# A fused linear attention and two feed-forward layers: products of halves for the second layer's second quarter, and a plain last group

## The chip, the cores and the metric

The kernel runs on one core of one Trainium2 chip. The metric is the device time of one execution in microseconds, from the profiler; several executions are timed and the median is taken. A core has TensorE (matrix products), VectorE (DVE), ScalarE (ACT), GpSimd (POOL), and SyncE (SP), which issues most transfers. Results of TensorE arrive in PSUM, eight banks of 512 columns of float32; all else is held in SBUF.

## The reference, cut to what matters

```
kv  = einsum('bhsd,bhse->bhde', k, v);  out = einsum('bhsd,bhde->bhse', q, kv)
out = out / sqrt(mean(out*out) + 1e-6) * g_norm          # 4 x 8 x 576 x 64
x   = out as 2304 tokens x 512
x   = softplus(x @ w_in1) @ w_out1                       # 512 -> 2048 -> 512
y   = elu(x @ w_in2) @ w_out2                            # 512 -> 2048 -> 512
```

All is float32. The weights come as float64 words and are rebuilt in the kernel.

## The kernel before, in words

**Numbers.** Every operand of a large product is held in two parts, a high one rounded to TensorE's fp32r type and a low one with the rest. A product is three matmuls: high x high, low x high and high x low. So each operand costs ScalarE a rounding copy and VectorE a subtraction.

**Tiling.** The 2304 tokens are six blocks of T = 384, taken as three pairs p. The hidden 2048 columns are four quarters q of four chunks of 128. A slot is two chunks for a pair (`slots`, 48 in all, 24 per layer), a group is the two slots of one quarter and pair. A group has a product into the hidden layer, an activation, and a product into the output, whose result is added to `acc_sb`.

**Products of halves.** A pair of blocks by two chunks is a 2 x 2 matrix of halves. The kernel forms it with seven products for eight (Strassen's scheme in Winograd's form): sums of operands are made beforehand, and three PSUM banks (A, B, C) collect the products. Into the hidden layer this is done almost everywhere (`product`, L874, products 1 to 7 of 6 matmuls of 384 columns each). Into the output it is done where `by_sevens(layer, q)` says so: before the change in the first layer from the second quarter on, in the second layer from the third on (SEVENS_FROM = 2). Elsewhere the output is plain (`slot_piece`, L1363 to L1365): in the second layer, 3 matmuls of 512 columns per chunk and tile of 128 tokens.

**A slot in sevens** (`slot_sevens`, L1117 to L1145, `part_sums`, L1157 to L1159). After the activation (`elu`, L1061 to L1081) h of the first block is split into x (768 columns, operands 1 and 2); of the second block x4 is split (384), S1 is formed, then three more sums of 384, and the two pairs of sums, xj and xk, are split (768 each). A plain slot splits only h of each block into G (768 each, `slot_parts`, L1322 and L1324).

**Output in sevens** (`out_piece`, L1216). Order of the products in the second layer: 1, 2, 6, 5, 3, 7, 4, each in two halves of rows m (two tiles, then one) and two slots f. A `fork` copies A into C (L1233, ScalarE). Six `flush` steps per half add a bank to `acc_sb` (L1250) or, in the last quarter, make the output o in one of three buffers q, which is sent out (L1248, L1258). Banks: A from a ring of two (`accA`), C and B from a ring of two (`accT`).

**Weights** (`conv`, L374 to L387; `split`, L404 and L408; `split_pair`, L460 to L466; `split_sums`, L474 to L483). A chunk is loaded, rebuilt and split; for products in sevens two chunks are combined: four VectorE operations of 256 columns, then two casts and two differences. The combined b12 takes the place of the original.

**The order.** It is written out by hand: the string TABLE names, step by step, a strand and the engine that takes its next step. Each engine runs its steps in the order of the list, so a wait on one engine holds all that the list puts behind it there. The strand `main` has the letters p (products into the hidden layer) and q (pieces into the output).

Of the kernel before, what the change touches and what calls it, by code (L numbers as in the profile page):

```python
# [17 lines left out]
P = 128  # L18
# [98 lines left out]
59p59p59p3qt3pt45t3pt46t47t3qt59p59p59p59p59p3pp3pa3pa59p48p3rt59p3qp48a3qa3qa59p59p48d59p3rt3st  # L117
3st00t48g59p59p3rp49p49a3ra3ra48d49d48p3sp4ap59p49g3tt3tt57t57t4ct4et4dt02t3ut4aa3sa3sa00a59p59p
59p4bp00a4ba59p59p49d4ad00d00d4bd00d59p49p4ag4bg59p59p59p59p3tp48a49a3ma3ta3ta01a59p59p59p59p4fp
3ut3vt02a4fa02a4ad5ad4bd01d4fd59p3vt3wt59p4bp4ap58p3up02d4fg3wt4ba4aa3ma3ua3ua3vp4gp02d02d4fd03a  # L120
4ga3va3va4fp3wp04t4jt03d4gd4fa3wa4gg4hp3wd5bd4ha04a4ip4ia04a58p4hd4hg4gd4id04d4gp4mp04d4hd4ig4ga
4ma4md04d4kt3xt3xt3yt3yt06t4qt4lt08t4np4hp4ha4na3ma06a06a59p59p4id4nd5cd58p3yp4ip58p4op4ia3ya3ma
5da5da05a5da4oa59p4mg4md06d3nd06d5ed06d05d3nd4od08a08a3ya07a4mp59p58p59p58p58p58p3zt3zt40t40t4rt
0at4ng4og40p08d4nd08d07d08d5dd4od3nd5ga40a40a09a5ga4np58p4up4tp4op58p58p58p0aa4ua4na0aa4ta4oa4ma
3na5ha3ma4pt0ct42t42t41t41t5at4ud09d0ad4td0ad58q4ug4tg0ad4ud5id4td58q58q58p58p4up3ma5ha0ca0ca4ua
0ba5ga42p4sp58p4sa58p5kd5jd0cd0bd42d0cd4sd0cd4sg0et5it44t43t44t43t42a5ha3na5la3na5la0ea0da0ea5hd
5md4sd5gd0ed0ed0dd4tp58q58q58p58p4sp58p4sa4ta3ma44p58p51t52t5bt0gt5mt53t0ed44d5od5nd44a58q54p55p
58q58q0fa54a3ma55a0fd54d54g5qd55d3nd5fd54d58q58q58q5pa55g58p58p58q54p58q0ga0ga5pa5la3na54a0gd55d
5sd5fd5fd5et5nt4vt58q55p56p58q58p58p5ra56a55a5pa5fa56d5ld0gd5wd56g58q4yp58q5va4ya56d4yd4yg58p56p
58p5ta5va5xa5ua5va56a0gd5pd5vd4yd4wt5st0jt5wt4xt0kt58p4zp58p4yp58q5fa0ja0ja4za4ya0ia5fa58q58q50p  # L130
58q5zd0jd4zd0jd50a0jd50d58q5ya5ya0ka0ka4zg50g60d4zd5fd0kd50d5zt60t0nt5kt5jt58q58p58p58q4zp58q58q
50p58q58p58p58q58q58q58q5fa4za50a3ma62a63a61a5ya58q0kd0kd65d66d3md3kd3md3md3kd3kd3kd5yd3kd3kd58q
58q58p67a64a3ma3ma3ma61a3ma68a68a3ma66t65t5qt58q58q58q58q6bd6ad68d6cd68d6dd3ld3md58q58q58q58q58q
58q58q58q58q58q6fa3ka6ga6ha69a58q58q58q58p58p61a3ma6ja58p58p58p6na6ia3ld3kd3ld6ed3ld6ld6kd3ld3ld
58p58p6pa6pa6oa3la58q58q58q58q58q61d6pd6pd0id3ld0hd0hd6rd6md0hd0hd58p58q58q58q6at6ct6dt6bt0ot3mt
6et6lt58q58p6qa6qa6qa6ta6ta0ha6ua58p58q58q58q58q58p58p6xa6sa6za6sa71a6qd6td0hd6wd6td6vd70d3mt3mt
3mt3mt58p58p0ma0na0na72a6ya58q58q58q58q58q58p58q58p0md6sd0nd0nd74d0nd0ld0ld76d0ld0ld75a73a73a73a
75a78a78a58p58p58p58q58q3mt3mt0rt78d75d78d0oa77a7aa0la0oa7ba79d73d58p58p58q0od0od7dd0ld0od58p58q
58q58p58q58q58q58q58q58p7ca77a7ca7ca0ra0ra7ea7ha77a7ga7ia0rd7cd0rd0rd7cd77d7jd0st3mt3mt0vt3mt3mt
58q58q58q58p58q0sa0sa7ka7la0qa77d0sd0sd77d0sd0qd0pd0pd77d0pd7fd0pd58p58p58q58q58q58q58q58p7oa7pa  # L140
77a7pa0pa7na7pa7na58q58q58q58q58p58p58q58q58q0wt3mt3mt3mt77d7qd0pd7nd7nd7pd7pd7ra0va7ka0va7ka0ua
7sa7ma7ta0vd0vd7kd0vd7md0ud58p58p58p58q58q0wa7ua0wa7va7za7ya80a7kd7kd0wd7xd0wd0wd0td7kd7wd58q58q
58p58q58p83a7ka82a84d0td0td7kd0td58q58p58q58p58p58q3mt0zt3mt86a7ta81a7ta85a85a0ta83a83a8aa8ag81d
87d85d85d0za0za89a58p58q58q58q58q8bd8cd0zd8dd0zd88d83d58q58p58q58q58p58q58q58q58q58q58p83d0td0zd
8hd8fd7td8id7td7td8kd7td8jd58q3mt10t8at3mt3mt58q58q58q8ga10a8ga10a8ea8ga0ya8ma89a8na58q58q58q58p
58p58p58q8ng7ta89a8la10d8gd10d8gd7td89d8ld8sd89d89d10d89d0yd8od8pa58q58q58p58p58q58q8qa8va89a8wa
8ua8xa0xd8rd89d0xd0xd0xd3mt3mt3mt13t58p58q58p58q58q58q58p8ya0xa8ya8ta8za8za93a91d90d92d8yd8yd0xd
8td58q58p58p58p58q58q58q58q58q58q58q58p13a13a12a95a96a8za8qa8qa9ba13d12d97d13d13d11d99d8zd94d11d
98d9ad8zd11d8qd8qd11d8qd8qd58q58p58q58q58q58q58p3mt3mt3mt3mt14t8nt9ea9ea9ca9ca8qa9fa9ga9gg58q58q
58p58q9hd9cd9cd9id9kd8qd58p58q58q14a14a9da95a95a14d14d9jd9md9dd95d14d58q58q58p58p58p58q58q3mt3mt  # L150
17t9gt9ea9pa9ra9la17a9qa9ed9nd9ed9od95d95d95d58p58q58q58q58p11a17a9sa9ua95a9ta9ta17d17d9vd95d9sd
17d11d58q58p58p58q58q58q58p58q58q3mt18t3mt9wa9la9la16a9za9xa18aa0a9ta18a9zg58q58q58p58q58p9ld16d
a1da2d18d9tda3d9yda4d9td18d9ld58p58p58q58q58q58q58q58q58q3mt3mt9zt3mt3mt1bt3mt9ld18d9lda8da7d15d
aada9d15d15d15da6aa0aa5a58q58q58q58q58q58q58p58p58q58p9laabaacaafa15aa6aacaa6aadd9ldabd15dacda6d
aeda6dacda0aaga1aaaha1ba1baaia1ada0d1bd1bd58q58p58p58qaigakaama3mt1ctaitajda0d1bda0da0d19d58q58q
58p58p58qaqd19d19d19dalaapaapaa0aanaaoaahaaraapaaraanda0dardard58p58p58p58q58q58q58qaha19aasa58q
58p58p58q58qava1ca1caayaawaawgapdahdaxd1cd1cd19dapdatdahdb0d1cd58q58p58q58q3mt3mt1ft3mt3mtawtb2d
58q58q58q58q58q58q58p1eab1aaua1fa1faazab1aahd1edb3db4d1fdb5d1fdahdb6d58q58q58q58q58p58q58qb1aaua
auab8ab9aahab7a1gt3mt3mtb9gb1db1daudbbdaud1fdahdaudaudb7dbaa1ga58p58q58q58p58q58q58p58pbga1gabca
bhaauabda1gdbed1gdbfd1gd1dd1dd1dd1dd58p58p58q58qb9t3mt1jtbiabkabmabjabja1dabldaudbjdbcd1ddbjd58p  # L160
58q58q58p58p58q58qbdabdabnabkaboa1ja1jabqabkabra58q58p58q58q58q58q58q58qbrgbta1iabdd1jd1jdbsdbkd
1idbvd1jdbudbpd1hdbkdbddbwd1hd1hd1hdbddbdd58q58p58p58p58q58q58q58q3mt3mt3mt3mt1kt3mt3mtbrtc0abxa
bzabxabda58q58q58p58qc1dc4dbxdbxdbddc6dc5d58q58q58p58p58p58q58q1kac0a1kabyabqabqa1hac7ac0acba1kd
1kd1kdbqdbyd1hdc2d1ntcbg58q58q58pcaac8accacda1nac3dc9dc0dc0dbqdbqdbqd58p58p58q58q58q1nachacfacea
bqa58q58q58pcgd1nd1ndbqdcedcid1ndc8acfac8acfacja1ma3mt1ot3mt58p58q58q58q58p58q58q58q58q58p1oa1oa
cqacfd1mdc8dcldcfdcmdcodcpdc8d1od1odckdc8d1od58q58q58q58q58q58p58p58p58q58q1ldc8d1ldcsd1ld1ldctd
3mt3mtcbt1rt3mt3mt3mt58q58qcvacnacuacyacyac8aczdcxdcydcwdcydc8d58q58q58q58q58pcra1ra1racna1lacna
d2acvad1a58p58p58q58p58qd0d1rd1ld1rdcrd1qad5acvad6a1rdcndd4d1qdcvd1pdcvdd5g58p58p58q58q58qd8ad3a
d9ad7adaad8a58p58qcnd1pdcndcnd1pd1pddbddcacnaddad8ad3adda58q58q58p58p58p58q1std5t3mt3mtdcdd8dcnd
ddddddd3a1padfa1sa1sadeadiadhadig58q58p58q58p58q58qdjad3d1sd1sd1sddkddgddmdd8dd3d1pd58p58p58q58q  # L170
58q58q58q58q58q58q1vt3mtdit3mt3mt3mtdodd3dd3ddqddpd58q3mt58q58q58qdnadna1ua1vadha1vadhadnadla1ud
dhd1vddrddsd1vddndduddnd1vddhddhd58q58q58q58q58q58p58p58pdxadyad3adtad3ddtddhddwadza58pdhae2adyg
dwd1tddvddhd1tde1d58p58p58q58q58q58p3oae0ae4ae4ae4ae5a1tde8d1tde4de7d58qe6ae9ae9ae3ae0ae0a58q58q
58q58p58q58q58pdyt1wte4d3ode9d3odecd3ode9dedde0deadebd58p58p58q58q58q58q58q58q58p1ta1wa3oa3oaefa
1waegaemdeldeed1wde0d1wdeidejdehd58p58p58q58q58q58q58qeka3oaena3oaepa3oaenae8temt1zte0derd1wdesd
eode0detd1tdeqaefae0aefa58p58q58q59p58qewd58q58q58p3odefde0dexdeyd58peqg58q1za1za1ya3oaeuaenaeva
# [57 lines left out]
def linear_attention_then_two_ffns(  # L234
# [857 lines left out]
    def slot_act(s, b, h, a):  # L1092
# [3 lines left out]
        if by_sevens(layer, q):  # L1096
            yield from slot_sevens(s, b, h, a)
            return
# [496 lines left out]
```

## Time and profile before

| | |
|---|---|
| runs | 790.48, 790.25, 790.72 us (median 790.48) |
| profiled execution | 790.45 us, its span from first to last instruction 788.7 us |
| TensorE clock granted | 1.00 throughout |
| TensorE, VectorE, ScalarE busy | 779.3, 663.7, 518.6 us |

How to read it: a busy time is the union of an engine's instructions. VectorE's and ScalarE's instructions overlap by some 0.08 us, so the spacing of starts is what one costs. Matmul ends are modelled; there too the spacing of starts counts. Windows give busy times per engine in a stretch, with the number of instructions in brackets.

### The profile page before, as it was taken

What the parts mean: (1) busy time and instruction counts of PE and PEld (TensorE: products, weight loads), DVE (VectorE), ACT (ScalarE), POOL (GpSimd) and SP (SyncE); (2) the same over time, 40 slices, a digit from 0 to 9 for tenths busy, and PEclk for the clock granted to TensorE, in tenths of its full rate; (3) what the DMA queues carried; (4) which work ended last, traced back from release to release, by engine and by line L of the source; (5) the groups of instructions that cost most, each with busy time, mean ns of one, the idle gap of its engine ahead of it and who ended that gap; (6) DMA issues with size and microseconds to landing.
All of it is one profiled execution on the core that took longest, in us unless ns stands there. A gap on an engine that the chain in (4) does not pass through costs nothing. (4 is left out here: it accounts for less than half of the span.)

```text
span 788.7 us, 13125 instructions
## 1 busy us (share of the span) xinstructions
PE 779.3 (99%) x4898; PEld 752.1 (95%) x4898; DVE 663.7 (84%) x1186; ACT 518.6 (66%) x984; POOL 57.1 (7%) x62
## 2 busy tenths in 40 slices
PE   8999999999999999999999999999999999999997
PEld 7899999999999999999998988998999999999996
DVE  3888887788889998999999996665778999999885
ACT  4877766676665676585677896765656767667551
POOL 3633500000000000000000000000000000000000
PEclk9999999999999999999999999999999999999999
DMA  9877799768678688779363879486674675685522
GB/s 321 292 269 294 250 376 319 276 241 290 223 232 301 212 279 288 242 227 309 121 215 143 284 294 322 173 301 224 216 254 154 247 254 180 262 293 181 174 81 86
DMA packets 49519, 191.30 MB, mean 243 GB/s; under 512 B 5296, under 2 KB 10928, under 8 KB 49456
## 3 DMA queue, kind: packets, MB, share of 16 engines
q1 hardware_dynamic: 47296, 184.57, 65.5%
q0 software_dynamic: 2160, 5.90, 4.1%
q8 instruction: 38, 0.62, 0.3%
q14 instruction: 25, 0.20, 0.1%
HBM read 146.80 MB, written 37.75 MB: 234 GB/s over the span
## 5 line engine op out<-in xcount | busy, mean ns | idle before, releaser
L874 PE MATMUL A<-x,wx 128*128 128x384 f32 x528 | 106.3, 335 | 0.0
L874 PE MATMUL A<-x,whi 128*128 128x384 f32 x352 | 99.9, 335 | 0.6 <-ACT hk L957 0.6
L874 PEld LDWEIGHTS A<-x,wx 128*128 128x128 f32 x528 | 92.4, 188 | 1.6 <-issue 0.3
L874 PEld LDWEIGHTS A<-x,whi 128*128 128x128 f32 x352 | 64.6, 188 | 1.4 <-ACT hk L957 0.9
L874 PE MATMUL A<-x,wlo 128*128 128x384 f32 x176 | 59.0, 335 | 0.0
L1365 PE MATMUL acc<-wlo,G 128*128 128x512 f32 x144 | 56.6, 393 | 0.0
L1364 PE MATMUL acc<-whi,G 128*128 128x512 f32 x144 | 56.6, 393 | 0.0
L1363 PE MATMUL acc<-whi,G 128*128 128x512 f32 x144 | 56.0, 389 | 0.0
L374 ACT ACTIVATE c<-raw 128x512 f32<-128x512 f32 x64 | 43.2, 675 | 17.4 <-DVE wx L480 8.7
L874 PE MATMUL B<-x,wx 128*128 128x384 f32 x264 | 53.0, 335 | 0.0
L874 PE MATMUL B<-x,whi 128*128 128x384 f32 x176 | 51.8, 335 | 0.0
L874 PE MATMUL C<-x,whi 128*128 128x384 f32 x176 | 51.8, 335 | 0.0
L408 DVE TENSOR_TENSOR wlo<-q,whi 128x512 fp32r<-128x512 f32 x64 | 44.0, 687 | 8.0 <-ACT whi L404 7.9
L874 PEld LDWEIGHTS B<-x,wx 128*128 128x128 f32 x264 | 46.2, 188 | 0.3
L387 DVE CUSTOM_DVE_ANT_0 q<-c,r 128x1024 uint16<-128x1024 uint16 x64 | 44.0, 687 | 1.4
L382 DVE SCALAR_TENSOR_TENSOR c<-raw,c 128x512 uint32<-128x512 uint32 x64 | 44.1, 689 | 1.0
L404 ACT CAST whi<-q 128x512 fp32r<-128x512 f32 x64 | 39.6, 619 | 7.5 <-DVE q L387 4.1
L377 ACT ACTIVATE r<-raw 128x512 uint32<-128x512 uint32 x64 | 42.9, 671 | 1.1 <-DVE wx L483 0.8
L1216 PE MATMUL A<-x,whi 128*128 128x384 f32 x144 | 41.7, 336 | 0.0
L834 DVE TENSOR_TENSOR x<-acc_sb,x 128x768 fp32r<-128x768 f32 x38 | 36.2, 954 | 3.4 <-ACT x L804 3.3
L902 PE MATMUL A<-x,whi 128*128 128x384 f32 x128 | 37.0, 344 | 0.0
L1290 POOL DMA_DIRECT2D acc_sb<-s x15 | 13.3, 887 | 326.2 <-ACT s L1275 219.6
(252 smaller groups left out, 2209.2 us busy)
## 6 DMA issues: line engine op xcount, KB each, us to landing
x<-spill SPq DMA_DIRECT2D x126, 768.0 KB, 6.5
raw<-w SPq DMA_DIRECT2D x64, 512.0 KB, 4.6
spill<-x SPq DMA_DIRECT2D x42, 768.0 KB, 6.1
acc_sb<-kv SPq DMA_DIRECT2D x16, 512.0 KB, 5.6
acc_sb<-s POOLq DMA_DIRECT2D x15, 384.0 KB, 5.5
out<-o SPq DMA_DIRECT2D x12, 256.0 KB, 2.2
q<-qt SPq DMA_DIRECT2D x9, 256.0 KB, 5.8
q_late<-qt SPq DMA_DIRECT2D x9, 256.0 KB, 3.5
```

Of the source, the lines that this page charges most:

```text
L374: nc.scalar.activation(c.bitcast(F32), high_f, AF.Copy, scale=2.0**-112)
L377: nc.scalar.activation(r, low, AF.Copy, scale=2.0**-29)
L382: nc.vector.scalar_tensor_tensor(c, high, 0x80000000, c, op0=ALU.bitwise_and, op1=ALU.bitwise_or)
L387: nc.vector.tensor_tensor(q.bitcast(U32), c, r, op=ALU.add)
L404: nc.scalar.copy(hi, q)
L408: nc.vector.tensor_sub(lo, q, f32(hi))
L874: nc.tensor.matmul(bank[:, :T], w, x, start=start and i == 0, stop=stop and i == len(seq) - 1, skip_group_check=True,)
L902: nc.tensor.matmul(a[:, :T], w, x, start=half == 0 and i == 0, stop=half == 1 and i == len(seq) - 1, skip_group_check=True,)
L1216: nc.tensor.matmul(a, l, r, start=first and k == i == 0, stop=last and i == 2, skip_group_check=True)
L1363: nc.tensor.matmul(a, l[0], r[0], start=(u == 0), stop=False)
L1364: nc.tensor.matmul(a, l[1], r[0], start=False, stop=False)
L1365: nc.tensor.matmul(a, l[0], r[1], start=False, stop=(u == QF - 1))
```

## The change

The second layer's second quarter goes in sevens too (SEVENS_FROM = 1), with its two weight pairs combined. The very last group (second layer, fourth quarter, third pair) is made plain for its output (`sevens_in`). Since that quarter's weights are combined ones, a new strand `right_again` restores the original right half of the first chunk from b11 and the sum b12 - b11, splits it again and writes it where product 4 of the group before had its operand. The plain pieces of the last group take their columns from both chunks' halves, so a tile of 512 columns is two times 3 matmuls of 256. The last tile's sum is made in two halves, as plain last groups are. The ring `accT` of two banks becomes `accT0` and `accT1` of one bank each, for the halves m of copies C and product 5. A branch in `flush_rows` could add sums by GpSimd's transfers, but its set BY_TRANSFER_2 is empty. The list is new throughout: 3698 steps for 3610, with 1234 for 1180 of VectorE and 1003 for 982 of ScalarE. From the first piece of the second layer's second quarter to the last of its third, VectorE has 349 steps in the new list and 311 in the old; for the third quarter alone the old list has 176. After the last product into the hidden layer the new list has 36 pieces: products 7 and 4 of the group before (8), then 28 of the last group.

```
-    SEVENS_FROM = 2
+    SEVENS_FROM = 1
+    BY_TRANSFER_2 = ()
-    BANKS = {"h": 2, "accA": 2, "accT": 2, "m": 1, "o": 1}
+    BANKS = {"h": 2, "accA": 2, "accT0": 1, "accT1": 1, "m": 1, "o": 1}
+    def sevens_in(layer, q, p):
+        return by_sevens(layer, q) and (layer, q, p) != (LAYERS - 1, NQ - 1, NPAIR - 1)
+    def right_again(f):
+        fc = NF - QF + 2 * f
+        need = [("w", LAYERS - 1, fc, 1), ("wx", LAYERS - 1, fc, 1)]
+        yield ((DVE, dve(256)),), [ring("cr"[f]), *need]
+        t, t_h = sbuf("cr"[f], 1, f"right{f}")
+        (lh, ll, *_), wx = w_t[LAYERS - 1, fc, 1], wx_t[LAYERS - 1, fc, 1][0]
+        nc.vector.tensor_add(t[:, :256], f32(lh)[:, :256], f32(ll)[:, :256])
+        yield ((DVE, dve(256)),), []
+        nc.vector.tensor_add(t[:, 256:], f32(wx)[:, 0, 0, :], f32(wx)[:, 1, 0, :])
+        yield ((DVE, dve(256)),), []
+        nc.vector.tensor_add(t[:, :256], t[:, :256], t[:, 256:])
+        hi, lo = w_t[LAYERS - 1, fc + 1, 1][:2]
+        yield ((ACT, act(256)),), [("four", f), ("w", LAYERS - 1, fc + 1, 1)]
+        nc.scalar.copy(hi[:, :256], t[:, :256])
+        yield ((DVE, dve(256)),), []
+        nc.vector.tensor_sub(lo[:, :256], t[:, :256], f32(hi)[:, :256])
+        drop(t_h)
+        mark("right", f)
...
-        sevens = by_sevens(layer, q)
+        sevens = sevens_in(layer, q, p)
...
-                5: [ring("accT")],
+                5: [ring(f"accT{m}")],
...
+            if (layer, q, p, o) == (LAYERS - 1, NQ - 1, NPAIR - 2, 4):
+                mark("four", f)
...
-            yield ((ACT, act(width, True)),), [ring("accT")]
-            banks["C", m] = psum("accT", f"C{n_}")
+            yield ((ACT, act(width, True)),), [ring(f"accT{m}")]
+            banks["C", m] = psum(f"accT{m}", f"C{n_}")
...
+        tag = ("accA", f"accT{(k // 2 + b * layer) % 2}")[k % 2]
+        if layer and by_sevens(layer, q):
+            need += [("w", layer, fc // 2 * 2 + 1, 1)] + [("right", f)] * (u % 2 == 0)
...
+            for n, x in enumerate(range(w0, w1, DM // 2)):
+                wh, wl = w_t[layer, fc // 2 * 2 + x * 2 // DM, 1][:2]
+                y = slice(DM // 2 * (u % 2), DM // 2 * (u % 2) + DM // 2)
+                to = a[:, n * DM // 2 : (n + 1) * DM // 2]
+                for v, (g_, w_) in enumerate(((l[0], wh), (l[0], wl), (l[1], wh))):
+                    nc.tensor.matmul(
+                        to, g_, w_[:, y], start=u == n == v == 0, stop=u == QF - 1 and v == 2,
+                        skip_group_check=True,
+                    )
...
-            if by_sevens(layer, q):
+            if sevens_in(layer, q, p):
                 yield from out_sevens(layer, q, p)
```

## Rows read from the trace of the kernel before

**Rows 1.** The page, busy time, share and instructions of each engine.
```profile
PE 779.3 (99%) x4898; PEld 752.1 (95%) x4898; DVE 663.7 (84%) x1186; ACT 518.6 (66%) x984; POOL 57.1 (7%) x62
```

**Rows 2.** Windows by stage of layer two: PE, PEld, DVE, ACT, POOL busy; clock, DMA.
```profile
430.00:522.00 92.00, 92.00 (x460) 82.92 (x460) 70.45 (x118) 71.40 (x132) 0.87 (x1) 1.00 0.75 265
522.00:614.00 92.00, 92.00 (x463) 83.44 (x462) 67.94 (x124) 53.27 (x101) 0.00 (x0) 1.00 0.64 228
614.00:703.00 89.00, 88.90 (x610) 87.69 (x610) 87.37 (x169) 63.45 (x119) 0.00 (x0) 1.00 0.67 243
703.00:785.00 82.00, 79.88 (x580) 78.25 (x578) 70.49 (x132) 41.35 (x76) 0.00 (x0) 1.00 0.41 140
...
500.00:600.00 100.00, 100.00 (x501) 90.32 (x500) 68.83 (x121) 62.47 (x118) 0.00 (x0) 1.00 0.64 226
640.00:720.00 80.00, 79.90 (x565) 79.41 (x564) 78.36 (x155) 54.39 (x101) 0.00 (x0) 1.00 0.63 229
```

**Rows 3.** Waits of TensorE from 30 us on: us, times, longest.
```profile
PE A L1216 <- DVE xj L1159: 0.7, 1, 0.7
...
PE A L1216 <- DVE o L1248: 0.4, 1, 0.4
```

**Rows 4.** Timeline of TensorE: start, us, instruction; 512, then 384 and 256 columns.
```profile
599.61 0.39 PE L1363 MATMUL acc<-whi,G 128*128 128x512 f32 x1
...
600.29 0.39 PE L1363 MATMUL acc<-whi,G 128*128 128x512 f32 x1
...
747.34 1.21 PE L874 MATMUL A<-x,wx 128*128 128x384 f32 x6
...
779.48 2.32 PE L1216 MATMUL A<-wx,xk 128*128 128x256 f32 x18
```

**Rows 5.** Timeline of TensorE at the end, with the idle time before and its releaser.
```profile
760.77 0.51 PE L874 MATMUL B<-x,whi 128*128 128x384 f32 x2
...
768.46 0.39 PE L1216 MATMUL A<-whi,x 128*128 128x256 f32 x1 [0.44 <-DVE o L1248]
...
772.55 2.45 PE L1216 MATMUL A<-wx,xj 128*128 128x256 f32 x16 [0.69 <-DVE xj L1159]
...
783.99 0.28 PE L1216 MATMUL A<-whi,x 128*128 128x256 f32 x1
```

**Rows 6.** Groups by line and form: xcount | busy us, mean ns | idle before.
```profile
L477 ACT CAST wx<-t 128x256 fp32r<-128x256 f32 x26 | 10.5, 404 | 0.9 <-DVE t L464 0.8
L466 DVE TENSOR_TENSOR q<-q,t 128x256 f32<-128x256 f32 x24 | 10.2, 423 | 0.4
L1233 ACT COPY C<-A 128x512 f32<-128x512 f32 x6 | 3.4, 573 | 1.9 <-PE A L1216 1.9
```

**Rows 7.** The chain that ended last, and VectorE's last sums in the timeline.
```profile
782.76 2.25 DMA out<-o
...
785.10 0.42 DVE o L1248
...
784.28 1.25 DVE L1248 TENSOR_TENSOR o<-acc_sb,A 128x512 f32<-128x512 f32 x2 [1.94 <-PE A L1216]
```

**Rows 8.** Timeline of VectorE, back to back: 768, 256, 512, 256 columns, then 384.
```profile
704.32 0.95 DVE L1119 TENSOR_TENSOR x<-hj,x 128x768 fp32r<-128x768 f32 x1
705.18 0.42 DVE L460 TENSOR_TENSOR t<-q,q 128x256 f32<-128x256 f32 x1
705.52 0.68 DVE L1250 TENSOR_TENSOR acc_sb<-acc_sb,A 128x512 f32<-128x512 f32 x1
706.12 0.42 DVE L462 TENSOR_TENSOR t<-q 128x256 f32<-128x256 f32 x1
...
707.12 0.55 DVE L1071 SCALAR_TENSOR_TENSOR hk<-e,A 128x384 f32<-128x384 f32 x1
707.58 0.42 DVE L466 TENSOR_TENSOR q<-q,t 128x256 f32<-128x256 f32 x1
```

**Rows 9.** Windows of 20 us, the turn from the first layer to the second.
```profile
420.00:440.00 20.00, 19.41 (x103) 17.77 (x102) 20.00 (x34) 17.64 (x33) 0.87 (x1) 1.00 0.37 112
```

More of the change, by code (lines that the diff above doesn't have):

```diff
@@ L1243, in flush_rows @@
             old = {3: [("s2", g, m)], 7: [("p5", g, m)]}.get(o, [])
+            if (q, p, o) in BY_TRANSFER_2 and m == 0:
+                yield ((ACT, act(width, True)),), [ring("f"), *old]
+                r, r_h = sbuf("f", 1, f"f{n_}_{o}")
+                r = r[:, :width].rearrange("p (t n) -> p t n", n=DM // 2)
+                nc.scalar.copy(r, x)
+                if name:
+                    mark(name, g, m)
+                if done:
+                    drop(x_h)
+                yield ((POOL, ADDS),), []
+                yield ((DMA, 2 * dma(P * width * 4)),), []
+                nc.gpsimd.dma_start(to, r, accum_op=ALU.add)
+                drop(r_h)
+                return
             yield ((DVE, dve(width)),), [ring("q"), *old] if ends else old
@@ L1348, in slot_piece @@
         fc = q * QF + u
-        tag = "acc" + "AT"[k % 2]
+        tag = ("accA", f"accT{(k // 2 + b * layer) % 2}")[k % 2]
         need = [("g", s, b), ("w", layer, fc, 1)] + [ring(tag)] * (u == 0)
-        yield ((PE, 3 * pe(w1 - w0)),), need
+        if layer and by_sevens(layer, q):
+            need += [("w", layer, fc // 2 * 2 + 1, 1)] + [("right", f)] * (u % 2 == 0)
+            yield ((PE, 3 * ((w1 - w0) // (DM // 2)) * pe(DM // 2)),), need
+        else:
+            yield ((PE, 3 * pe(w1 - w0)),), need
         gh, gl, G_h = g_t[s, b]
         hi, lo, hi_h, lo_h = w_t[layer, fc, 1]
+        halves = layer and by_sevens(layer, q)
         if u == 0:
@@ L1362, in slot_piece @@
             l, r = (gh[:, c], gl[:, c]), (hi[:, w0:w1], lo[:, w0:w1])
+        if halves:
+            for n, x in enumerate(range(w0, w1, DM // 2)):
[7 more added lines that the diff above has]
+                    )
+            if k == len(cut) - 1 and b == 0 and u == QF - 1:
+                mark("ended")
+            piece_done(s, b, f, k, u, i, w0, w1, cut, acc, left, G_h, layer, q, p)
+            return
         nc.tensor.matmul(a, l[0], r[0], start=(u == 0), stop=False)
@@ L1365, in slot_piece, with piece_done @@
         nc.tensor.matmul(a, l[0], r[1], start=False, stop=(u == QF - 1))
+        piece_done(s, b, f, k, u, i, w0, w1, cut, acc, left, G_h, layer, q, p)
+        if p == NPAIR - 1 and b == (layer == q == 0 and PLAIN == NPAIR) and k == len(cut) - 1:
+            drop(hi_h)
+            drop(lo_h)
+    def piece_done(s, b, f, k, u, i, w0, w1, cut, acc, left, G_h, layer, q, p):
         left[f] -= 1
@@ L1369, in slot_piece @@
                 drop(h)
-        if p == NPAIR - 1 and b == (layer == q == 0 and PLAIN == NPAIR) and k == len(cut) - 1:
-            drop(hi_h)
-            drop(lo_h)
         if u == QF - 1:
@@ L1531, in linear_attention_then_two_ffns @@
             order.add(AGAIN_KEY[f], pair_again(f))
+        for f in range(FP):
+            order.add(base(LAYERS * SLOTS - 2) + 1.5, right_again(f))
         for layer in range(LAYERS):
```

239 lines of the change are left out of this document (121 added, 118 removed).

## The prediction

> **What bounds the kernel now.** I read the busy times first: TensorE is busy for 99% of the span, VectorE for 84%, ScalarE for 66% [rows 1]. A busy TensorE need not be at its peak, so the windows by stage come next. The second layer's quarters run from about 430, 522, 614 and 703 us [rows 2]. In the first two, with plain products into the output, VectorE works 70.45 and 67.94 of 92 us; in the third, in sevens, 87.37 of 89, and TensorE still has no hole there (88.90 of 89). In the table of TensorE's waits the longest after the start is 0.7 us [rows 3], and what it loses lies mostly in the last 25 us: the fourth stage has 79.88 of 82 us. So the time is the number of columns that TensorE must stream, plus what it loses at the end; VectorE stands close behind.
>
> **The price of a matmul.** Starts of the 512-column matmuls of plain pieces are 0.23 us apart; three of them take 0.68 us, 0.227 each. Eighteen 256-column matmuls of sevens span 2.32 us, the last one's 0.28 included: 0.120 each. Six of 384 span 1.21 us, or 0.175, the last one's 0.34 included [rows 4]. Cost goes with columns.
>
> A plain group in the second layer has 2 blocks x 4 chunks x 3 tiles x 3 = 72 matmuls of 512: 16.3 us. A group in sevens has 7 products x 2 slots x 3 tiles x 3 = 126 of 256: 15.1 us. The windows agree: with its 84 matmuls into the hidden layer a plain group is 156, and 501 in 100 us make 31.1 us for one; a group in sevens is 210, and 565 in 80 us make 29.7 [rows 2]. The three groups of the second quarter gain 3 x 1.25 = 3.75 us. The last group becomes plain, but its pieces are cut in halves: 144 matmuls of 256 for 126, so 18 x 0.120 = 2.15 us more. **Columns: 1.6 us gained.**
>
> The Trainium skill, "TensorE: Matmul & The Clock Gate", section "Back-to-back issue gap", speaks against the change: it gives sustained spacings of about 81 ns for 128 columns and 131 ns for 512, so that long matmuls are the cheap ones. As an estimate from that page, on a straight line between, 256 columns would take 98 ns, a group 9.4 us plain and 12.3 us in sevens, and the columns' sum would be a loss of about 10 us. The rows have 0.227 and 0.120 us, so here the measured spacing decides and the page's does not apply.
>
> **The end.** After the last product into the hidden layer, which ends at about 761.1, TensorE still runs 165 matmuls of 256 (39 of the group before, 126 of the last one), and the last one starts at 783.99 [rows 5]. 165 x 0.120 is 19.7 us of the 23.0: 3.3 are lost. Two gaps have a name, 0.69 us for VectorE's split of the sums xj and 0.44 us for an output sum; the rest are small waits for sums that free a bank. With the last group plain these parts are not made: no x4, S1, three sums and two splits of sums per slot, and its matmuls need only G of a block. What takes their place is `right_again`: in the new list the plain group's first piece needs ("right", 0), which needs product 4 of the group before, half 0, then ScalarE's 256-column copy and VectorE's 256-column difference. A 256-column cast takes 0.404 us, a 256-column VectorE operation 0.42 [rows 6], and with a handover of about 0.1 after each the next piece starts 1.2 us after that product; the one piece left of product 4 covers 0.36 us. So 0.85 us stand free, and I allow 0.25 for a second wait; ends 0 (the list puts other ready pieces there) and 3.3 (as much as now). **2.2 us gained.**
>
> Then the tail. VectorE's last two sums wait for room in the three q buffers: one starts at 784.28 and the last not before the transfer of an earlier output lands at 785.01, so it starts at 785.10, 0.8 us behind the end of the last matmul (783.99 + 0.28) [rows 7]. In the plain group outputs come 2.9, 2.9 and 1.45 us apart (24 or 12 matmuls each), a transfer takes 2.25, and the buffer that the last one needs is free by then. **0.8 us gained**, ends 0 and 0.8.
>
> **VectorE in the second quarter.** Its prices are start to start: 768 columns 0.87 us, 512 0.60, 384 0.47, 256 0.335 [rows 8]. A plain slot has 6 operations of 384 (c22, c12, four of the ELU) and 2 of 768; a slot in sevens has 12 and 3. That is 6 x 0.47 + 0.87 = 3.7 us more, 7.4 a group. The six sums of 512 (3.6 us) become six of 512 and six of 256 (5.6). So a group costs 9.4 us more, three 28.3. The two weight pairs of the quarter, now combined, cost 2 x (4 x 0.335 + 0.60 + 0.335) = 4.6. Together 33 us, where VectorE works 67.94 of 92 us. That does not fit into 88.5 us; part must move to the neighbours, of which the first quarter has 21 us free. ScalarE gets two forks (one of 512 columns takes 0.57 us) per group and the combined weights' casts, against 39 us free [rows 2, 6].
>
> Unknown is what TensorE loses when VectorE is full for two quarters on end. From below: nothing. In the third quarter VectorE is 98% busy and TensorE loses 0.1 us. From above: a quarter in sevens needs 49.4 us for six slots, 16.9 for sums, 17.1 for eight weight chunks, 9.1 for four pairs and about 1 for copies, 93.5 in all against TensorE's 88.5, so 5 us a quarter and 10 in all if nothing moves. A row between: at 420 to 440 us VectorE is busy for all 20 us and TensorE is busy for 19.41, losing 0.6 us in plain sight [rows 9]. Between the first piece of the second quarter and the last of the third the new list has 349 VectorE steps; at the third quarter's 87.37 / 169 = 0.517 us a step that is 180.4 us beside 177 of TensorE. For the third quarter alone the old list has 176 steps, 91 us by the same price beside 88.5, and that excess of 2.5 was carried without a loss. The new excess is 3.4 over twice the time. I take **1.5 us lost**, nearer to the third quarter's row than to the inventory; ends 0 and 10.
>
> **Priced at nothing.** The banks: a ring of two handed round in one order becomes two rings of one, in the same order, so a copy and product 5 of the same half follow one another as before. The weights' transfers move the same bytes in shorter runs, with the DMA engines 64% busy in that stage; cover gone, a late chunk would show as ScalarE waiting on raw, and VectorE and then TensorE behind it. SP issues one output transfer fewer (23 for 24). The transfer branch for sums is not taken, its set is empty, so POOL's queue gets nothing. The new list may move anything else by some tenths either way.
>
> **Sum.** -1.6 - 2.2 - 0.8 + 1.5 = -3.1 us. The profiled execution took 790.45 us (span 788.7), against a median of 790.48, so the sum holds for both: **787.4 us**. A measurement can tell about 0.2%, 1.6 us, from no change.
>
> **The rivals.** (1) VectorE loses nothing: the list spreads its work into the first quarter. Then 785.9. The slack there and the third quarter speak for it, the 0.6 us at 420 against it. (2) VectorE becomes the bound, the other side: from the point where its lateness costs TensorE over 6.2 us (4.6 gained and 1.6 more) the kernel is slower. With the inventory's 10 us it is 790.5 - 4.6 + 10 = 796; at 7 it is 793. The place is the second quarter's end and the third, where the splits x, xj and xk come late and the input of each product waits. For it: 93.5 over 88.5 us in two quarters running. Against it: the list's 349 steps. The Trainium skill, "Perfetto Trace Analysis", section "Optimizing Scalar/DVE Operations", says that with VectorE saturated work should be offloaded to ScalarE; the change keeps all sums on VectorE, and what that costs no run here shows. (3) The same lateness costs 3 to 6 us and eats the gain: 789 to 791.5. (4) The end does not get shorter, since `right_again` waits for product 4 at the point where nothing else is ready: 787.4 + 2.2 = 789.6. That the change does less than it says I rule out: the pieces and their matmuls follow from the code.
>
> **Chances.** Forecast (a loss of 0.5 to 3 us at VectorE, 786.4 to 788.9) 0.41; rival 1 0.25; rival 3 0.15; rival 4 0.05; rival 2 0.14. Faster is the forecast and rival 1: 0.66. Within 0.2%: rivals 3 and 4, 0.20. Slower: 0.14. The range goes from 784.6 (rival 1 with the wait on `right` covered, and some tenths from the list) to 792.2 (rival 2's near edge).
>
> **What would show it.** Right: 256-column matmuls up by 3 x 126 + 144 - 126 = 396, 512-column ones down by 216; VectorE busy for 97% or more from 522 to 700 and TensorE windows there without holes of more than 1.5 us together; after the last product into the hidden layer 180 matmuls with about 1 us lost; a last sum that waits for a matmul and not for a transfer. Wrong: TensorE waiting for x, xj, xk or for a sum's bank all through the second and third quarters; a wait of over 2 us on whi behind `right_again`; a chain at the end that still runs over output transfers.

## The result, and the profile after

| | before | after |
|---|---|---|
| median (runs) | 790.48 us (790.25 to 790.72) | 797.15 us (796.90 to 798.69) |
| ratio, 95% interval | | 1.0086 [1.0071, 1.0102] |
| profiled execution, span | 790.45, 788.7 us | 796.90, 795.1 us |

The change makes the kernel slower, by 6.7 us (0.7 to 1.0%). First the page of the kernel after, its busy times, against [rows 1]; then its windows by stage, against [rows 2, 9] (same columns), with two short stretches at turns of quarters behind them.

```profile
PE 781.3 (98%) x5082; PEld 760.6 (96%) x5082; DVE 685.0 (86%) x1240; ACT 529.4 (67%) x1005; POOL 55.9 (7%) x62
```

```profile
430.00:522.00 92.00, 90.85 (x455) 81.89 (x456) 73.75 (x124) 70.27 (x132) 0.87 (x1) 1.00 0.78 278
522.00:614.00 92.00, 91.17 (x618) 89.11 (x617) 89.58 (x174) 66.85 (x125) 0.00 (x0) 1.00 0.64 240
614.00:703.00 89.00, 86.99 (x610) 85.83 (x609) 87.40 (x171) 62.66 (x118) 0.00 (x0) 1.00 0.57 204
703.00:785.00 82.00, 80.01 (x573) 78.38 (x572) 68.27 (x130) 42.72 (x79) 0.00 (x0) 1.00 0.46 168
...
420.00:440.00 20.00, 18.51 (x103) 17.43 (x102) 20.00 (x34) 16.36 (x31) 0.87 (x1) 1.00 0.64 221
616.00:628.00 12.00, 9.99 (x67) 8.86 (x66) 11.79 (x24) 10.14 (x19) 0.00 (x0) 1.00 0.41 153
716.00:724.00 8.00, 6.30 (x38) 5.44 (x38) 7.73 (x17) 5.77 (x10) 0.00 (x0) 1.00 0.35 106
```

VectorE now works 89.58 of 92 us in the second quarter (67.94 before), and TensorE, which had hardly a hole from 440 to 703 us, has them in every stage, 2.0 and 1.7 us in the two short stretches alone. Its waits from 30 us on (us, times, longest), which had no more than 0.7 us in one place [rows 3]:

```profile
PE A L1245 <- DVE acc_sb L1296: 2.1, 4, 1.0
PE A L903 <- ACT hk L986: 1.3, 1, 1.3
PE A L1245 <- DVE wlo L416: 0.9, 2, 0.6
PE A L1245 <- ACT whi L412: 0.8, 1, 0.8
PE A L903 <- ACT hj L986: 0.7, 2, 0.5
```

**Where the time went.** To place it, the pitches of [rows 4] are added up over all matmuls up to a moment (0.227, 0.172 and 0.120 us for 512, 384 and 256 columns; the shorter ones of the attention by their own pitch) and taken from the time of that moment; what is left is lost. "Streamed" is that sum at the end, and "760 on" stops at the last matmul's start. The pitches set the level of every column: with the mean spacings of back-to-back matmuls in these two traces (0.229, 0.174 and 0.119 us) some 5 us less is lost between 100 and 760 us in either, and 8.8 us lie between the two kernels where the table has 8.2. So the differences carry the argument, to some 0.6 us, and not the levels.

```
us lost            up to 100   100-420  420-460  460-520  520-600  600-700  700-760   100-760   760 on   streamed
before                 11.45      2.78     1.78     0.89     1.22     1.24     0.19      8.10     3.25      761.2
after                  14.59      2.84     3.21     1.00     2.10     3.80     3.34     16.29     1.00      759.6
```

The profiled executions differ by 6.45 us: columns -1.6, start +3.1, from 100 to 760 us +8.2, the end -2.25, and what follows the last matmul -1.0 (3.69 for 4.67 us). The gains are as forecast, though the columns' -1.6 is the forecast's own pitches times the counts (-2.3 by the mean spacings). The loss in the middle is over five times its term. By place it is 1.4 us from 420 to 460, 3.4 from 520 to 700, 3.2 from 700 to 760, and 0.2 in the rest.

How a hole of the middle comes about, at the turn into the third quarter: first the timeline of TensorE, then of VectorE.

```profile
615.77 1.84 PE L1245 MATMUL A<-wx,xk 128*128 128x256 f32 x14
...
619.09 0.28 PE L1245 MATMUL A<-whi,x 128*128 128x256 f32 x1
620.35 0.38 PE L1245 MATMUL A<-whi,x 128*128 128x256 f32 x1 [0.99 <-DVE acc_sb L1296]
```

```profile
616.94 0.69 DVE L1296 TENSOR_TENSOR acc_sb<-acc_sb,A 128x512 f32<-128x512 f32 x1 [0.21 <-PE A L1245]
617.54 0.42 DVE L468 TENSOR_TENSOR t<-q,q 128x256 f32<-128x256 f32 x1
617.88 0.55 DVE L1110 SCALAR_TENSOR_TENSOR hj<-e,hj 128x384 f32<-128x384 f32 x1
618.35 0.42 DVE L470 TENSOR_TENSOR t<-q 128x256 f32<-128x256 f32 x1
618.68 0.95 DVE L1188 TENSOR_TENSOR xj<-hj,xj 128x768 fp32r<-128x768 f32 x1
619.55 0.42 DVE L472 TENSOR_TENSOR t<-q,t 128x256 f32<-128x256 f32 x1
619.88 0.41 DVE L1296 TENSOR_TENSOR acc_sb<-acc_sb,A 128x256 f32<-128x256 f32 x1
620.22 0.42 DVE L474 TENSOR_TENSOR q<-q,t 128x256 f32<-128x256 f32 x1
```

TensorE has finished a piece by 619.4 and needs a bank A for the next; the bank comes free with the sum at 619.88. What that sum adds is there by about 617.6 (14 matmuls of 0.120 from 615.77, and the last one's 0.28), but it stands in VectorE's list behind five others, three of them (L468, L470, L472) of a weight pair that is being combined. After the first row none has idle time before it: VectorE does not rest, and the list decides who is late. The Trainium skill, "PSUM — Partial Sum Buffer", section "Engine vs sequencer instructions", says that VectorE's and ScalarE's queues are strictly first in, first out; the rows agree: a sum of 0.33 us waited for 2.3 us of other work ahead of it.

Not every hole is VectorE's alone. The longest wait of the table above, 1.3 us on the copy of hk (L986), ends at 430.7 us, at the turn between the layers, and names ScalarE; the waits on whi and hj name it too:

```profile
430.73 0.44 PE L903 MATMUL A<-x,whi 128*128 128x384 f32 x1 [1.30 <-ACT hk L986]
```

The end, against [rows 5, 7]: the timeline of TensorE (the last product into the hidden layer, the first and the last piece of the plain group), then VectorE's last sums.

```profile
768.70 0.51 PE L903 MATMUL B<-x,whi 128*128 128x384 f32 x2
...
773.98 0.35 PE L1421 MATMUL acc<-whi,G 128*128 128x256 f32 x1 [0.15 <-ACT whi L494]
...
791.44 0.28 PE L1421 MATMUL acc<-whi,G 128*128 128x256 f32 x1
```

```profile
790.32 0.42 DVE L751 TENSOR_TENSOR o<-acc_sb,acc 128x256 f32<-128x256 f32 x1 [0.75 <-PE acc L1421]
791.76 0.42 DVE L751 TENSOR_TENSOR o<-acc_sb,acc 128x256 f32<-128x256 f32 x1 [1.01 <-PE acc L1421]
```

### The profile page after: what moved, and what is told of

It is laid out like the page before. It is cut to its first block, busy times and chain, and to the rows that moved or that the text cites. A ratio compares the mean times of both kernels' runs of the same rounds, so it can differ in the third digit from the quotient of the medians.

```text
span 795.1 us, 13586 instructions
## 1 busy us (share of the span) xinstructions
PE 781.3 (98%) x5082; PEld 760.6 (96%) x5082; DVE 685.0 (86%) x1240; ACT 529.4 (67%) x1005; POOL 55.9 (7%) x62
## 4 chain that ended last, share of the span: by engine, by line
PE 86%; DVE 9%; ACT 1%; DMA 1%; issue 1%; SPq 0%; DVEq 0%
PE A L903 20%; PE A L1245 15%; PE B L903 10%; PE B L1245 8%; PE C L903 5%; PE A L931 4%; PE C L1245 4%; PE acc L1429 4%; PE acc L1431 4%; PE acc L1430 4%; PE acc L1421 2%; PE kv L579 1%; PE po L646 1%; PE warm L1546 1%; DVE x L863 1%
## 5 line engine op out<-in xcount | busy, mean ns | idle before, releaser
L1245 PE MATMUL A<-whi,x 128*128 128x256 f32 x192 | 39.9, 287 | 3.2 <-DVE acc_sb L1296 2.1
L986 ACT COPY hk<-A 128x384 f32<-128x384 f32 x37 | 17.7, 479 | 33.8 <-PE A L903 33.6
L1245 PEld LDWEIGHTS A<-whi,x 128*128 128x128 f32 x192 | 31.6, 189 | 5.5 <-DVE acc_sb L1296 3.6
```

The source lines that it names most:

```text
L1245: nc.tensor.matmul(a, l, r, start=first and k == i == 0, stop=last and i == 2, skip_group_check=True)
```

## The experiments

Each experiment had the kernel before beside it on the same chip; ratios are to that. The table gives for each profiled execution what it lost, as above. Four rows lose 0.19 to 0.21 us from 700 to 760 us; every kernel with the plain last group loses 1.2 us or more there.

```
us lost                        up to 100   100-520  520-600  600-700  700-760   100-760   median   before beside it
before                             11.45      5.45     1.22     1.24     0.19      8.10   790.48
after                              14.59      7.05     2.10     3.80     3.34     16.29   797.15   790.48
last group plain alone             14.04      5.44     1.27     0.92     1.21      8.84   791.36   790.61
old order up to 200 us             11.57      7.23     2.09     3.77     3.33     16.42   794.05   790.61
less work for VectorE              13.10     10.04     1.39     2.22     3.03     16.68   794.96   790.61
one ring of two banks              13.91      7.74     2.10     3.78     3.33     16.95   796.55   790.61
list c                             14.14      7.06     1.08     3.25     1.45     12.84   791.77   791.74
list d                             12.86      5.36     1.46     2.90     1.52     11.24   790.30   791.72
list d, less work                  11.52      5.12     0.37     0.69     1.39      7.57   785.95   791.72
before, 10 us more for VectorE     12.88      5.72     2.91     0.93     0.20      9.76   793.45   791.74
before, 21 us more                 14.55      5.40     7.47     2.74     0.20     15.81   800.31   791.74
before, 31 us more                 13.75      5.40    10.64     8.44     0.21     24.69   808.27   791.74
```

**The last group plain, alone.** TensorE's order of the kernel before up to the last 36 pieces, that of the change from there, and the banks in one ring. On VectorE and ScalarE the order departs from that of before earlier, from some 733 us on, and VectorE takes the first steps of `right_again` at 735 us.

```
-    SEVENS_FROM = 1
+    SEVENS_FROM = 2
-    BANKS = {"h": 2, "accA": 2, "accT0": 1, "accT1": 1, "m": 1, "o": 1}
+    BANKS = {"h": 2, "accA": 2, "accT": 2, "m": 1, "o": 1}
...
```

> The last group plain alone: the second layer's second quarter stays plain, accT is a ring of two again, the old list is kept up to the last 36 pieces and the new list's order is taken from there. If the end does what the two traces say (2.15 us more columns, 2.25 less lost after the last product into the hidden layer, 1.0 less after the last matmul), the time is 790.5 + 2.15 - 2.25 - 1.0 = 789.4 us. Rival: the shorter end is a gift of the emptier VectorE queue of the whole new list; then the columns alone count and the time is 791.5 to 792.6.

791.36 us, ratio 1.0004 [0.9995, 1.0014]. Its profile has the three parts as expected: 763.3 us streamed (+2.1), 0.99 lost from 760 us on (-2.26), 3.68 after the last matmul (-1.0), so -1.2. But it also loses 1.02 us more from 700 to 760 us, so that all these together come to -0.1, and in the median no gain shows: the interval, -0.4 to +1.1 us, excludes -1.2. The rival's 791.5 to 792.6 is nearer than the expected 789.4. In front of the holes, at 739.6, 741.3 and 748.1 us, VectorE's list has the first steps of `right_again`:

```profile
735.29 0.75 DVE L484 TENSOR_TENSOR right<-whi,wlo 128x256 f32<-128x256 f32 x2
```

That these steps cause the holes was not tested; a few copies changed places there as well.

**The old order at the start.** The changed kernel, the list of the kernel before for the first 200 us. In this run and that of one ring below some banks come to hold other sums than the reference's; all instructions and sizes are those of the change.

```
-    BANKS = {"h": 2, "accA": 2, "accT0": 1, "accT1": 1, "m": 1, "o": 1}
+    BANKS = {"h": 2, "accA": 2, "accT": 2, "m": 1, "o": 1}
-    TABLE (the list of the change)
+    TABLE (the list of before up to 200 us, then that of the change)
...
```

> The changed kernel with the old list's order for the first 200 us and the new order behind it; accT as a ring of two, since the old order hands its banks round in another way than one bank per half allows. If the 3.1 us that TensorE loses more in the first 60 us come from the new list's start, the time falls from 797.15 to 794 us, and the loss at 100 us from 14.6 to 11.5. Rival: they belong to the execution or the chip, and the time stays within 0.5 us of 797.

794.05 us, 1.0042 [1.0027, 1.0056], and the 3.1 us at the start were gone, as expected. By itself this run would put them down to the list. The table speaks against that: with the old order at the start eleven profiled executions (lists a and b below, which have no line in the table, among them) lost 11.45 to 14.55 us up to 100 us, with the new one three lost 13.10 to 14.59. The times of all executions lean the other way: the five of this run took 793.71 to 794.55 us, while the seven of the changed kernel and of the run with one ring, in the new order throughout, took 794.34 to 798.89, six of them over 796. Whether the new order makes a bad start more frequent stays open. What does stand: from 100 us on this run loses 16.4 us like the changed kernel, and with a start like that of before the change costs 3.4 us.

**Less work for VectorE.** In the second layer the low parts of the weights and of x, x4, xj and xk are products with nought, so they hold no low values; VectorE has some 30 us less. One of the six places, and the function that three of them call:

```
+    def low(s, to, h, hi):
+        if slots[s][0]:
+            nc.vector.tensor_scalar(to, hi, 0.0, None, op0=ALU.mult)
+        else:
+            nc.vector.tensor_sub(to, h, hi)
...
-        nc.vector.tensor_sub(parts[1], h, f32(parts[0]))
+        low(s, parts[1], h, f32(parts[0]))
...
```

> The changed kernel, same list, with some 30 us of VectorE work taken out of the second layer: the low parts of weights, x, x4, xj and xk are written as the high part times zero (one input, about half the time) and not as a difference, so the low parts are zero. If VectorE's load as such delays TensorE, the 9 us lost from 420 to 760 us fall below 3 and the time is 789 to 791 us. Rival: the order of the list does, at the turns from quarter to quarter, where steps wait for matmuls and rooms in front of steps that TensorE needs; then most of the loss stays and the time is 793.5 to 796 us.

794.96 us, 1.0048 [1.0029, 1.0067]. From 520 to 760 us it loses 6.64 us, for 9.24 in the changed kernel and 2.65 before. (Between 290 and 305 us it lost 3.6 us otherwise: 1.8 in a wait for a transfer of x, and most of the rest behind it at the lower level of the clock, 1.2 GHz for 2.4; the table's 16.68 has it.) So over a third of what the change loses there went with 30 us of VectorE's work, most of it from 600 to 700 us, and the rest stayed although VectorE was now free for some 12 us in each of the second and third quarters:

```profile
522.00:614.00 92.00, 91.82 (x623) 89.84 (x622) 79.40 (x177) 66.95 (x127) 0.00 (x0) 1.00 0.67 246
614.00:703.00 89.00, 88.23 (x621) 87.32 (x621) 77.68 (x174) 62.22 (x118) 0.00 (x0) 1.00 0.58 208
```

The time is the rival's (793.5 to 796). This is the stretch at the lower level, with the granted clock of 0.50:

```profile
296.00:299.00 3.00, 3.00 (x11) 3.00 (x10) 1.87 (x4) 1.28 (x3) 0.00 (x0) 0.50 0.47 194
```
 The part of the loss that stayed points to the order of the list.

**One ring of two banks.** The changed kernel and its list, with accT0 and accT1 as one ring again.

```
-    BANKS = {"h": 2, "accA": 2, "accT0": 1, "accT1": 1, "m": 1, "o": 1}
+    BANKS = {"h": 2, "accA": 2, "accT": 2, "m": 1, "o": 1}
...
```

> The changed kernel and its list with accT as one ring of two banks. If the split of the banks has a price of its own, the time falls by 1 us or more below 797. If a ring of two handed round in this list's order is the same as two rings of one, as the prediction priced it, the time stays at 796.5 to 798 us.

796.55 us, 1.0073 [1.0050, 1.0095], and the losses by stage are those of the changed kernel to 0.1 us from 460 us on. The split of the banks has no price that shows.

**Two searched lists, a and b.** With the banks of the change, and the transposed tile of the attention in the bank that the old order wants for it:

```
-            tag = ("accA", f"accT{nm // 2 % 2}")[nm % 2] if j < 3 else "om"[nm % 2]
+            tag = ("accA", "accT0")[nm % 2] if j < 3 else "om"[nm % 2]
...
-            yield from late(nm, bank, po_h, x, tag)
+            yield from late(nm, bank, po_h, x, "accT1" if tag == "accT0" else tag)
-    TABLE (the list of the change)
+    TABLE (the list of before up to 200 us, then a searched order)
```

> The changed kernel with another list: the order of the kernel before for the first 200 us, and from there an order searched for this kernel, in which the weights' conversions of the second layer are taken earlier and the sums of products stand ahead of them. Every operation of the changed kernel is still made, on the same engines but for some ten steps; the banks stay one each. VectorE's load from 520 to 702 us is as in the changed kernel. Theory (the list, not the load): the losses of the changed kernel at the start (3.1 us), at the turn between the layers (1.5) and in the second to fourth quarters (7.7, against 2.65 in the kernel before) mostly go: 785 to 788 us. Rival (a VectorE that is full for two quarters on end costs TensorE, whatever the order): only the start is won back, 793 to 794.5.

> As the run beside it, with a third order of the same steps, reached from another start of the search. It says how far one list differs from another. Theory (the list, not the load): within 2 us of the run beside it, 785 to 789 us. Rival (the load): 793 to 795.

830.15 us, 1.0478 [1.0444, 1.0512], and 818.10 us, 1.0317 [1.0302, 1.0333]: the theory and the rival of either run miss by far. The waits of ScalarE between 220 and 780 us, first in list a, then in list b and in the kernel before:

```profile
ACT c L382 <- DMA raw<-w: 66.7, 21, 6.8
```

```profile
ACT c L382 <- DMA raw<-w: 60.0, 19, 6.0
```

```profile
ACT c L374 <- DMA raw<-w: 7.0, 3, 3.8
```

Both lists convert a weights' chunk right behind the issue of its transfer, which lands some 5 us later. The page of list a, its DMA issues (count, KB each, median us from issue to landing):

```profile
raw<-w SPq DMA_DIRECT2D x64, 512.0 KB, 5.0
```

ScalarE stands there, and all that the list puts behind it stands too.

**List c.** The same edit, with an order in which each transfer has its time.

> Again the changed kernel with another list and every operation of it (the list of the kernel before for the first 200 us, three steps of VectorE more and three of ScalarE fewer than in the changed kernel). The two lists tried so far took the weights' chunks too soon after their transfers were issued: ScalarE waited 66.7 us for raw, where the kernel before has 7.0. This list leaves every transfer 2.7 us beyond its own length before its reader's place. VectorE's work between the stages is moved by a few us only: about 4 more before 520 us, 1 less from 520 to 612, 5 less from 702 on. Theory (the order, not the amount): 786.5 to 789.5 us, under the kernel before. Rival (VectorE full for two quarters on end costs TensorE its 6 to 7 us in any order): 792 to 794, only the start won back.

791.77 us, 0.9994 [0.9982, 1.0007]: level with the kernel before, where the changed kernel was at 1.0086. From 100 to 760 us it loses 12.84 for 16.29 us. Both expectations miss: 791.77 is 0.2 us under the rival's 792 to 794 and 2.3 over the theory's 789.5. They were reckoned from 790.5 us for the kernel before, though, which took 791.74 beside this run. Against it the theory was 1 to 4 us faster and the rival 1.5 to 3.5 slower, and level lies between them.

**VectorE's work by itself.** The kernel before with its own list, and a repeated difference in the 12 steps of the second quarter that make G's low parts (REP is 2, 3 and 4; a repeat writes the same values).

```
-        nc.vector.tensor_sub(gl, h, f32(gh))
+        for _ in range(REP if 30 <= s < 36 else 1):
+            nc.vector.tensor_sub(gl, h, f32(gh))
```

> The kernel before with VectorE loaded more in the second layer's second quarter, and its list as it is: the difference that gives the low part of G (768 columns, 0.87 us) is taken twice in each of the 12 steps, 10.4 us more for VectorE. Theory (that quarter has 92 - 68 = 24 us free, but in pieces between steps that others wait for): up to 1.5 us slower. Rival (any work put in front of the sums is paid at once): 4 us or more.

> The same with the difference taken three times, 20.9 us more, so that VectorE has 89 of 92 us. Theory: 4 to 7 us slower, since an order made for a quarter with VectorE at 74% cannot carry 97%. Rival (VectorE's amount of work counts only once it passes TensorE's): under 1.5 us.

> The same with the difference taken four times, 31.3 us more, about what the change adds there (33). Theory: 10 to 13 us slower in the order of the kernel before; the changed kernel carries as much for 6 to 8 with its own order, so an order of its own is worth some 4 us there already. Rival (the excess over the quarter's free 24 us alone is paid): 7 to 8 us.

Ratios 1.0016 [1.0006, 1.0027], 1.0105 [1.0089, 1.0120] and 1.0203 [1.0183, 1.0223], or 1.3, 8.3 and 16.1 us. The first has the time expected; the other two cost more than theory (4 to 7 and 10 to 13) and rival alike. Placed here, the first 10 us are nearly free, and each further one costs some 0.7. The windows of the second quarter with 10, 21 and 31 us more:

```profile
522.00:614.00 92.00, 91.20 (x455) 81.76 (x454) 75.79 (x131) 52.79 (x100) 0.00 (x0) 1.00 0.61 216
```

```profile
522.00:614.00 92.00, 86.02 (x420) 75.32 (x419) 79.58 (x127) 49.75 (x93) 0.00 (x0) 1.00 0.57 203
```

```profile
522.00:614.00 92.00, 80.52 (x381) 71.24 (x381) 81.56 (x126) 44.21 (x83) 0.00 (x0) 0.96 0.51 186
```

In the last one the mean granted clock is 0.96. At two places TensorE ran partly at the lower level, 1.2 GHz for 2.4: from 531 us on, behind a wait of 2.29 us, and from 606 us on, behind one of 2.42. Two rows of the first, where six matmuls of 384 take 1.21 us otherwise [rows 4], and the window of the second:

```profile
531.75 2.29 PE L874 MATMUL B<-x,wx 128*128 128x384 f32 x6 [2.29 <-DVE hj L967]
533.83 1.82 PE L874 MATMUL A<-x,wx 128*128 128x384 f32 x6
```

```profile
606.00:611.00 5.00, 4.84 (x18) 4.51 (x18) 4.90 (x7) 3.13 (x6) 0.00 (x0) 0.66 0.00 0
```

The twelve matmuls lost 1.7 us by it, and 0.34 of 5 us are as much again. So some 3 us of the last step's 7.8 are, in this profile, the clock's price of the rests and not the lateness itself.

With 21 us more TensorE has 6 us of holes while VectorE still rests for 12 of 92. The quarter's free 24 us were not free where they were needed. The Trainium skill, "Perfetto Trace Analysis", section "Optimizing Scalar/DVE Operations", speaks of VectorE causing bubbles on other engines without being saturated, and says that breaking up instructions may then let work be completed sooner; these rows agree with the first, and the second no run here shows. For a saturated VectorE, where the prediction has "should be offloaded", the Trainium skill says in that section only that offloading some work may make sense; no run here shows what it would do.

**List d, and list d with less work.** List c worked on further at the places where TensorE still stood; the second kernel has the edit of the less work besides (no low values in the second layer).

> The changed kernel with the list of the run before it worked on further, step by step, at the places where TensorE stood in it (a copy on ScalarE for a product's third bank at 626 us, a sum at 720, the restored weight at 762). Every operation is made. Theory (most of the loss is the order): 0.5 to 2 us below the kernel before. Rival (what the list before it still lost, 12.8 us between 100 and 760 us against 8.1, is the price of VectorE being full and does not go): within 0.7 us of the kernel before.

> The same list, and in the second layer the low parts are products with nought (one operand) in place of differences (two), so that the parts hold no low values there; VectorE gets some 10 us free in each of the second and third quarters, as in the run of the changed kernel where this was done first. If what this list still loses is VectorE's amount of work: 2 us or more below the run beside it. If it is other waits (copies on ScalarE, transfers): within 1 us of it.

List d: 790.30 us, 0.9982 [0.9972, 0.9992], under both kernels. With less work: 785.95, 0.9930 [0.9916, 0.9944]. Both came out as expected, 0.5 to 2 us under the kernel before and 2 us or more under list d. The windows of list d, then with less work:

```profile
430.00:522.00 92.00, 92.00 (x465) 83.61 (x464) 77.39 (x132) 67.83 (x127) 0.87 (x1) 1.00 0.77 275
522.00:614.00 92.00, 91.58 (x631) 90.00 (x630) 89.99 (x173) 66.78 (x126) 0.00 (x0) 1.00 0.65 229
614.00:703.00 89.00, 87.70 (x614) 86.57 (x613) 88.20 (x171) 62.37 (x118) 0.00 (x0) 1.00 0.63 219
```

```profile
522.00:614.00 92.00, 92.00 (x642) 91.42 (x641) 81.86 (x178) 67.45 (x129) 0.00 (x0) 1.00 0.65 230
614.00:703.00 89.00, 88.97 (x628) 88.76 (x627) 79.57 (x174) 63.41 (x120) 0.00 (x0) 1.00 0.65 229
```

In one and the same order TensorE has 1.7 us of holes in two quarters with VectorE at 98 and 99%, and none with it at 89%. (The cheaper operations also shorten each split, 0.95 us to 0.55, so amount and delay of a single step are not told apart.) From 100 to 760 us the loss goes from 16.29 (the change) to 11.24 by the list, in which three steps also went from ScalarE to VectorE, and to 7.57 with less work too, the level of before (8.10). So of the 8.2 us that the change loses there, 5.0 went with another order; the other 3.1 went with less work of VectorE, and whether a still better order would take them too is not shown.

By place the two differ. From 520 to 700 us, where VectorE is full, the change loses 5.90 us, with less work 3.61; list d 4.36, with less work 1.06; the kernel before 2.46. There less work takes away 2.3 and 3.3 us, the order 1.5 and 2.5. Outside these two quarters list d loses 3.5 us less than the change.

## Why the prediction was wrong

The forecast was 787.4 us and faster; measured were 797.15 and slower, outside the range. Of the 9.8 us between them 6.7 are the term for VectorE and 3.1 the start; the other terms came out as forecast.

**Columns: right.** There are 396 more matmuls of 256 columns and 216 fewer of 512, as counted, and 256 columns still start 0.120 us apart (14 in 1.84 us at 615.77). That is -1.6 us by the forecast's pitches (-1.5 as they are printed) and -2.3 by the mean spacings. The loss of about 10 us, an estimate from the Trainium skill's spacings ("TensorE: Matmul & The Clock Gate", "Back-to-back issue gap"), did not come.

**The end: right behind 760 us.** 2.2 forecast, 2.25 measured. 180 matmuls of 256 follow the last product into the hidden layer, and 1.0 us is lost; the wait on `right_again` is 0.15 us at 773.98, where I had allowed more. What it left out is that `right_again` takes VectorE's time earlier: the plain last group alone loses 1.0 us more from 700 to 760 us, and does not gain in the median.

**The tail: right.** 0.8 forecast, 1.0 measured; the last sum waits for a matmul, as foretold.

**Priced at nothing.** The banks: right, by the run with one ring. "The new list may move anything else by some tenths": the start was 3.1 us longer in the profile, and whether that belongs to the list or to the execution stays open.

**VectorE in the second quarter: wrong, and this is the step that failed.** I gave 1.5 us, since the third quarter of before carried an excess of 2.5 us at 98% without a loss, and 349 steps at its mean price came to only 3.4 us more than TensorE's time. Measured are 8.2 us, near the upper end of 10. That VectorE would be full was right (89.58 of 92 and 87.40 of 89 us, almost what the third quarter had before). What failed is the inference from one list to another. In the two quarters that the term was about the loss is 3.4 us for 1.5; list d, with VectorE at 99% in the third, also loses 2.90 us from 600 to 700 us where the kernel before loses 1.24. So 98% without a hole went with the order of before, and a mean price of steps tells nothing of when each is due.

The larger part, 4.7 us, lies at the turns before and behind these quarters, which "the new list may move anything else by some tenths" put at nothing, without a row. Over the whole middle 5.0 us went with another order of nearly the same steps, and 3.1 with less work.

**Slack counted by quarter was the other fault.** "Part must move to the neighbours, of which the first quarter has 21 us free" takes idle time as a store. The repeated differences show that of the second quarter's 24 free us some 10 could be used in the old order, and past those 0.7 of each us came out at the end. Usable room is the order's: list d puts 77.39 us of VectorE's work into the first quarter, 6.9 more than before, and TensorE has no hole there (92.00 of 92).

**The rivals.** The second one has the outcome, slower by over 6.2 us of lateness, but its mechanism only in part: of the 8.2 us 3.4 lie in its place, the second and third quarters. Without the start's 3.1 us the change would stand at 793.8 by the profile, inside its 793 to 796, and that is luck as far as the place goes. The holes stand at turns, 420 to 440, 530 to 560, 616 to 628 and 716 to 724 us; at the later ones a new quarter's weights are converted and combined between the sums. The 0.6 us at 420 to 440 us [rows 9] and the inventory's 93.5 over 88.5 us had spoken for it and were set aside.

The list of the change, more than the products of halves, is what made it slower than before: with list d the same products, banks and plain last group beat the kernel before by 1.4 us (0.6 to 2.2 by the interval). That is still 1.7 us short of the forecast, and list d has the old order at the start too.

## What to carry to other kernels

A neighbour stage that runs full without a hole shows that its own order carries this, not that another stage in another order can be filled as far: price added work on a busy engine by the steps it stands ahead of, and by a run that repeats some existing instruction there, which shows how much of the idle time is usable. Where the order is written out, a structural change and its order are two changes; compare structures only with an order made for each. An order must give every transfer its time to land: two that did not, with 60 and 67 us of ScalarE's waits for weights, came out 25 and 38 us slower than the kernel before.

## What the runs showed of the hardware that was not expected

The start differs from execution to execution by 3 us in the same, old order. TensorE waits there for k and v (1.0 us in the kernel before, 2.2 in the changed one), and behind such rests its granted clock can fall. Windows of 2 us, the changed kernel, then the kernel before with 10 us more for VectorE, which has the old order there, then the run with the old order up to 200 us, where it did not fall:

```profile
6.00:8.00 2.00, 0.60 (x17) 0.42 (x13) 0.00 (x0) 0.00 (x0) 0.00 (x0) 1.00 1.01 323
8.00:10.00 2.00, 2.00 (x14) 2.00 (x12) 0.00 (x0) 0.41 (x2) 0.00 (x0) 0.60 1.04 348
10.00:12.00 2.00, 2.00 (x25) 1.66 (x25) 0.55 (x1) 0.59 (x2) 0.22 (x1) 0.54 0.95 322
```

```profile
6.00:8.00 2.00, 1.31 (x23) 0.94 (x19) 0.00 (x0) 0.41 (x2) 0.00 (x0) 1.00 1.08 342
8.00:10.00 2.00, 2.00 (x18) 1.77 (x20) 0.34 (x1) 0.49 (x1) 0.00 (x0) 0.66 1.05 342
10.00:12.00 2.00, 2.00 (x22) 1.88 (x19) 0.21 (x1) 0.41 (x2) 1.61 (x2) 0.50 1.04 346
```

```profile
6.00:8.00 2.00, 1.26 (x21) 0.89 (x18) 0.00 (x0) 0.41 (x2) 0.00 (x0) 1.00 1.03 326
8.00:10.00 2.00, 2.00 (x30) 1.81 (x31) 0.55 (x1) 0.67 (x2) 0.00 (x0) 1.00 0.99 340
```

A mean of 0.5 to 0.66 is mostly the lower level, 1.2 GHz for 2.4. TensorE had been busy for 0.60 and 1.31 of the 2 us before in the two executions where it fell, and for 1.26 in the one where it did not, so these windows do not tell when it falls. It fell at the start in four of the fourteen profiled executions (the first two here, that with one ring and that of list d), and later, once or more, in four others (less work, lists a and b, and 31 us more). A mean of 0.57 over 4 us, as in the first two groups of rows, is at most 1.7 us lost. Executions without it lost up to 14.55 us at the start, so it is not the whole of the spread. Nothing of it was priced. Two kernels that differ by 1 us need many runs.
